# A long convolution with a two-layer MLP: batch 1's second transform stage as four 64x64 products, its spectrum product on VectorE through PSUM, and the pair sums on GpSimd

## The chip, the cores and the metric

The kernel runs on one core of a Trainium2 chip. The metric is the time of one execution on the device in microseconds (us), measured from launch to end. Engines are named as the profile names them: PE (TensorE's matmuls), PEld (its weight loads), DVE (VectorE), ACT (ScalarE), POOL (GpSimd), SP (SyncE, which issues most DMAs here). PSUM is the accumulator memory that PE writes; DVE and ACT read and write it.

## The reference

For two batches of 12480 tokens with 128 channels it computes a causal convolution along the sequence with a filter made by a small MLP from position embeddings, multiplies by x, and runs a two-layer MLP over all 24960 tokens:

```python
h_filt = (np.maximum(pos_emb @ w1, 0.0) @ w2) * window
u = x * v
y = np.fft.irfft(np.fft.rfft(u, n=2*S, axis=1) * np.fft.rfft(h_filt, n=2*S, axis=0), n=2*S, axis=1)[:, :S]
a = (x * y).reshape(B * S, D)
h = a @ w_in
out = np.maximum(0.01 * h, h) @ w_out
```

## The kernel before

**The convolution** is a two-stage Fourier transform over a sequence of 98 x 128 points. Stage one works along 98 points (matmuls with tables `ft`), stage two along 128 points, which `mb` splits into two halves s = 0, 1 of 64 outputs each. Stage two works on 25 *chunks* of up to four frequencies k (4 x 128 channels = 512 columns; the 13th chunk falls into two pieces, the last has 256 columns). In each chunk the forward transform gives the spectrum, it is multiplied by the filter's spectrum `hspec`, and an inverse transform along the same axis gives `ct`, which goes to DRAM (`scr2`). The last inverse stage is part of the MLP's front: for a pair of rows (a *tile* t of 390 tokens) `join_hi` (L673) and `join_lo` (L687) form sums and differences `cp`, matmuls `yp` (L933) transform them, and transposes, products with x and a split into a high and a low part make the MLP's input `zh`, `zl`.

**Order of the program.** Batch 0 goes through its two stages first (to about 340 us). Then the MLP runs in *slots*: 50 column blocks k times 16 blocks f of the hidden layer, 800 slots. In each slot `m1` issues three matmuls (L1009, a high and low split in place of one fp32 product) into one of three PSUM banks `mh`; ACT makes `rh` (L1013), DVE makes `rl` (L1014), and `m2`, three slots later, issues three matmuls (L1050 to L1052). Every engine runs its own instructions in the order in which the program issues them.

**Batch 1's convolution is laid between the MLP's slots.** `conv1` (stage one) and `conv1b` (stage two) are generators; after each slot `pace` calls them for as many *pieces* as a straight line asks for, so that they end a few slots before batch 1's first tile. So each `yield` in `conv1b` is a place where MLP instructions come between. Before, one chunk of `conv1b` has 15 pieces, about 1.5 a slot, and a chunk comes every 9 to 10 slots.

**One chunk of `conv1b` before.** The input is split into a high part (ACT, L507 and L511, `th`) and a low part (DVE, L512, `tl`). The forward transform takes six matmuls of the full array (L150 in `three`: for each s, high by high, low by high, high by low) into two PSUM banks `cv` that are obtained by `psc["next"]`. ACT copies both banks with the halves exchanged (L551, L558), DVE multiplies the banks by `hspec`'s real part (L553), POOL multiplies the exchanged copy by the imaginary part and adds (L517, L518). ACT and POOL split the product again (L575 `ph`, L576 `pl`). One chunk later `back` issues six more matmuls (L150) into the same two banks, and ACT copies the result out (L230 in `mixed_evac`). There are only two `cv` buffers, so a chunk's inverse transform, the other user, can start only when the forward result of the chunk in hand has been read.

`join_hi` forms the upper-half sums of a pair with DVE for t = 0 and for batch 0's tiles from 8 on, and with POOL for the others.

Of the kernel before, what the change touches and what calls it, by code (L numbers as in the profile page):

```python
# [8 lines left out]
F32 = mybir.dt.float32  # L9
F32R = mybir.dt.float32r  # L10
# [11 lines left out]
MC1 = 4  # L22
# [8 lines left out]
def tile_conv_mlp(ctx, tc, x, v, pos_emb, w1, w2, w_in, w_out, cf, cr, cg, cb, ci, cw, out):  # L31
# [20 lines left out]
    hspec = dram.tile([NCH, HB, 2, 2, 512], F32, name="hspec")  # L52
# [11 lines left out]
    mb_h = const.tile([128, 2, 128], F32R, name="mb_h")  # L64
    mb_l = const.tile([128, 2, 128], F32R, name="mb_l")
    mi2 = [const.tile([128, 2, 128], F32, name=f"mi2{j}") for j in range(2)]
    mi_h = [const.tile([128, 2, 128], F32R, name=f"mi_h{j}") for j in range(2)]
    mi_l = [const.tile([128, 2, 128], F32R, name=f"mi_l{j}") for j in range(2)]
# [78 lines left out]
    def three(dst, a, b):  # L147

        for i, (u, w) in enumerate(((a[0], b[0]), (a[0], b[1]), (a[1], b[0]))):
            nc.tensor.matmul(dst, u, w, start=(i == 0), stop=(i == 2))  # L150
# [16 lines left out]
    def even(w):  # L167

        return (w.stop - w.start) // D % 2 == 0

    def back(dp, parts, c):

        for s in range(2):
            for j, w in halves(c):
                m = mixed if even(w) else lambda t: t
                three(dp[s][:, w], (mi_h[j][:, s], mi_l[j][:, s]), (m(parts[0][:, s, w]), m(parts[1][:, s, w])))

    def turned(pool, psum, m2, m1):
# [36 lines left out]
        nc.scalar.copy(mi_h[1], rp[:, 2:4])  # L215
        nc.vector.tensor_tensor(out=mi_l[1], in0=rp[:, 2:4], in1=mi_h[1], op=ALU.subtract)
        yield

    def store_back(b, c, ct, eng):
        k0, n = chunk(c)  # L220
        eng.dma_start(out=scr2[b][k0:k0 + n].rearrange("k r m e -> (r m) k e"),
                          in_=ct[:, :n].rearrange("p k s d -> p k (s d)"))

    def mixed_evac(dp, ct, c):

        for s in range(2):
            for _, w in halves(c):
                o, i = ct[:, w.start // D:w.stop // D, s, :], dp[s][:, w]
                if even(w):
                    nc.scalar.copy(o.rearrange("p (h k) d -> p h k d", h=2),  # L230
                                   i.rearrange("p (k d h) -> p h k d", h=2, d=D))
                else:
                    nc.scalar.copy(o, i.rearrange("p (k d) -> p k d", d=D))
            yield
# [8 lines left out]
    with tc.manual_schedule():  # L243
# [22 lines left out]
        with ExitStack() as st:  # L266
# [86 lines left out]
            for c in range(NC0):  # L353
# [4 lines left out]
                if c == 2:  # L358
                    turn_ = turned(sba, lambda: psa.tile([128, 4, 128], F32, tag="pp", name="tp"), mi2[0], mi)
                    next(turn_)  # L360
                    nc.sync.dma_start(out=mb, in_=cb)
                    nc.sync.dma_start(out=mi, in_=ci)
# [3 lines left out]
                if c == 6:  # L366
                    nc.scalar.mul(mi, mi, 1 / 0.99)
                    for m, mh, ml in ((mb.rearrange("p s r q -> p s (r q)"), mb_h, mb_l), (mi, mi_h[0], mi_l[0])):
                        nc.scalar.copy(mh, m)
                        nc.vector.tensor_tensor(out=ml, in0=m, in1=mh, op=ALU.subtract)  # L370
# [60 lines left out]
        WAIT = 12  # L431
# [49 lines left out]
        def conv1b():  # L481
# [4 lines left out]
            def fetch_b(c):  # L486
                if c < NCH:
# [3 lines left out]
                    nc.sync.dma_start(out=got[c][:, :n].rearrange("p k s d -> p k (s d)"),  # L491
                                      in_=scr1b[:, k0:k0 + n, :])

            def fetch_h(c):
                n = chunk(c)[1]
                h = pool.tile([128, 2, 2, 512], F32, tag="hd", name="hd")
                for i in range(2):
                    nc.sync.dma_start(out=h[HB * i:HB * i + HB, :, :, :n * D], in_=hspec[c][:, :, :, :n * D])
                hd[c] = h

            def split(c):
                _, n = chunk(c)
                t = got.pop(c)
                th = pool.tile([128, KC, 2, D], F32R, tag="th", name="th", bufs=1)
                tl = pool.tile([128, KC, 2, D], F32R, tag="tl", name="tl", bufs=1)
                parts[c] = th, tl
# [810 lines left out]
```

## Time and profile before

| what | value |
|---|---|
| median of 3 runs | 1619.28 us (1616.59 to 1620.77) |
| profiled execution, its own time | 1622.39 us |
| its span, first to last instruction | 1620.6 us |
| PE busy | 1559.0 us, 96% of the span |
| DVE, ACT, POOL busy | 70%, 61%, 46% |
| mean granted clock of TensorE | 0.986 |

Busy time is the union of an engine's instructions. A matmul's record is longer than the distance to the next one, since matmuls are pipelined: the distances between their starts tell what PE is paid for.

### The profile page before, as it was taken

To read this page: it belongs to the slowest core of one execution; us is meant where nothing else is said; L and a number is where in the kernel's file an instruction comes from. 1 tells how busy PE (TensorE), PEld (TensorE's weight loads), DVE (VectorE), ACT (ScalarE), POOL (GpSimd) and SP (SyncE) were. 2 spreads that over 40 slices of the span, in tenths; PEclk is the share of its full clock that TensorE was granted. 3 is DMA by queue.
4 is the path that set the end of the run, shared out by engine and by line. 5 is a ranking of instruction groups with operands and counts; after the bars stand their busy time and mean duration, and the time that the engine had idled before them with its cause. 6 is when DMAs were issued, how large, how long until landed. Compare 5 with 4: busy or idle time off the path is not lost.

```text
span 1620.6 us, 27366 instructions
## 1 busy us (share of the span) xinstructions
PE 1559.0 (96%) x9173; PEld 1323.7 (82%) x9173; DVE 1129.5 (70%) x1785; ACT 995.9 (61%) x2108; POOL 748.6 (46%) x804
## 2 busy tenths in 40 slices
PE   6798899899999999999999999999999999999999
PEld 6787555478888888888888888988888888888888
DVE  4676687765777566666677775577777777777777
ACT  2232454435655466777776777677777776777776
POOL 4563121234735257677777775453433533334310
PEclk9899999999999999999999999999999999999999
DMA  8898999966676557666656752321212212122200
GB/s 247 266 297 264 309 318 324 326 177 200 199 200 200 154 155 195 192 181 181 170 164 179 194 141 63 110 95 57 77 58 63 68 63 87 58 63 62 63 11 21
DMA packets 166358, 253.31 MB, mean 156 GB/s; under 512 B 14302, under 2 KB 119026, under 8 KB 163146
## 3 DMA queue, kind: packets, MB, share of 16 engines
q1 hardware_dynamic: 146478, 226.29, 47.2%
q10 hardware_dynamic: 19740, 25.28, 4.6%
q8 instruction: 73, 1.20, 0.3%
q14 instruction: 67, 0.55, 0.1%
HBM read 168.00 MB, written 83.43 MB: 155 GB/s over the span
## 4 chain that ended last, share of the span: by engine, by line
PE 74%; DMA 9%; DVE 6%; ACT 3%; issue 2%; SPq 1%; POOL 1%; ACTq 0%; DVEq 0%; POOLq 0%
PE mh L1009 28%; PE acc L1051 9%; PE acc L1052 9%; PE acc L1050 9%; PE yp L933 4%; PE cv L150 3%; PE cv L454 3%; DMA scr<-ct 3%; PE op L1082 2%; PE zp L952 1%; PE up L136 1%; DMA pos<-in_pos_emb_dram 1%; PE dp L164 1%; DMA scr<-o 1%; PE a L410 1%
## 5 line engine op out<-in xcount | busy, mean ns | idle before, releaser
L1014 DVE SCALAR_TENSOR_TENSOR rl<-mh,rh 128x512 fp32r<-128x512 f32 (+1 forms) x336 | 226.7, 682 | 199.1 <-ACT rh L1013 197.9
L1022 DVE TENSOR_TENSOR rl<-mh,rh 128x512 fp32r<-128x512 f32 (+2 forms) x416 | 277.2, 670 | 83.6 <-ACT rh L1021 75.0
L1017 ACT ACTIVATE mh<-mh 128x512 f32<-128x512 f32 (+2 forms) x416 | 236.3, 568 | 154.0 <-PE mh L1009 113.3
L1009 PE MATMUL mh<-zh,w_in_h 128*128 128x512 f32 (+3 forms) x800 | 316.8, 396 | 3.6 <-DVE rl L1014 2.4
L1009 PE MATMUL mh<-zl,w_in_h 128*128 128x512 f32 (+3 forms) x800 | 300.0, 375 | 0.2 <-POOL zl L966 0.2
L1009 PE MATMUL mh<-zh,w_in_l 128*128 128x512 f32 (+3 forms) x800 | 299.6, 375 | 0.0
L1051 PE MATMUL acc<-rl,w_out_h 128*128 128x512 f32 (+3 forms) x800 | 299.1, 374 | 0.1
L1050 PE MATMUL acc<-rh,w_out_h 128*128 128x512 f32 (+3 forms) x800 | 299.0, 374 | 0.0
L1052 PE MATMUL acc<-rh,w_out_l 128*128 128x512 f32 (+3 forms) x800 | 299.0, 374 | 0.0
L1013 ACT ACTIVATE rh<-mh 128x512 fp32r<-128x512 f32 (+1 forms) x336 | 198.9, 595 | 133.1 <-PE mh L1009 124.3
L966 POOL TENSOR_TENSOR zl<-zf,zh 128x390 fp32r<-128x390 f32 (+24 forms) x110 | 67.8, 630 | 426.5 <-ACT zh L965 403.8
L696 POOL TENSOR_TENSOR cp<-cq,cp 98x256 f32<-98x256 f32 x248 | 194.0, 782 | 32.6 <-DVE cp L684 15.9
L1019 DVE CAST rh<-mh 128x512 fp32r<-128x512 f32 (+2 forms) x208 | 139.3, 670 | 65.9 <-ACT mh L1017 65.5
L1009 PEld LDWEIGHTS mh<-zh,w_in_h 128*128 128x128 f32 x800 | 151.7, 190 | 29.6 <-DVE rl L1014 8.7
L1009 PEld LDWEIGHTS mh<-zh,w_in_l 128*128 128x128 f32 x800 | 151.8, 190 | 19.7
L1051 PEld LDWEIGHTS acc<-rl,w_out_h 128*128 128x128 f32 x800 | 151.2, 189 | 20.2 <-DVE rl L1022 0.4
L1050 PEld LDWEIGHTS acc<-rh,w_out_h 128*128 128x128 f32 x800 | 151.2, 189 | 19.8
L1052 PEld LDWEIGHTS acc<-rh,w_out_l 128*128 128x128 f32 x800 | 151.2, 189 | 19.7
L1009 PEld LDWEIGHTS mh<-zl,w_in_h 128*128 128x128 f32 x800 | 152.2, 190 | 15.6 <-POOL zl L966 0.6
L1021 ACT CAST rh<-mh 128x512 fp32r<-128x512 f32 (+2 forms) x208 | 118.5, 570 | 6.5
L693 POOL TENSOR_TENSOR cq<-cin 98x256 f32<-98x256 f32 x124 | 97.6, 787 | 0.3 <-DMA cin<-scr 0.3
L105 ACT COPY a1s<-a 98x384 f32<-98x384 f32 x64 | 30.7, 480 | 97.3 <-PE a L410 68.7
(170 smaller groups left out, 2529.8 us busy)
## 6 DMA issues: line engine op xcount, KB each, us to landing
cin<-scr SPq DMA_DIRECT2D x318, 98.0 KB
hd<-hspec SPq DMA_DIRECT2D x48, 512.0 KB
bin<-scr SPq DMA_DIRECT2D x23, 768.0 KB
scr<-o SPq DMA_DIRECT2D x28, 588.0 KB
scr<-ct SPq DMA_DIRECT2D x25, 512.0 KB
scr1b<-o SPq DMA_DIRECT2D x32, 392.0 KB
hspec<-hs ACTq DMA_DIRECT2D x48, 256.0 KB
xm<-in_x_dram SPq DMA_DIRECT2D x128, 96.0 KB
```

Of the source, the lines that this page charges most:

```text
L693: eng.tensor_tensor(out=cq[:, p], in0=ci_t[:, 0, :, 0, :], in1=ci_t[:, 0, :, 1, :], op=op)
L696: eng.tensor_tensor(out=cp[:, p, w], in0=cq[:, p], in1=cp[:, p, 1], op=op)
L1009: nc.tensor.matmul(hp, u[:, fs], m, start=(i == 0), stop=(i == 2))
L1013: nc.scalar.activation(out=split2(rh), in_=plain(hp), func=AF.Relu)
L1014: nc.vector.scalar_tensor_tensor(out=split2(rl), in0=plain(hp), scalar=0.0, in1=split2(rh), op0=ALU.max, op1=ALU.subtract)
L1017: nc.scalar.activation(out=hp, in_=hp, func=AF.Lrelu, alpha=0.01)
L1019: nc.vector.tensor_copy(split2(rh), plain(hp))
L1021: nc.scalar.copy(split2(rh), plain(hp))
L1022: nc.vector.tensor_tensor(out=split2(rl), in0=plain(hp), in1=split2(rh), op=ALU.subtract)
L1050: nc.tensor.matmul(ap, w_out_h[:, f, :], rh, start=(f == 0 and not sums(k)), stop=False)
L1051: nc.tensor.matmul(ap, w_out_h[:, f, :], rl, start=False, stop=False)
L1052: nc.tensor.matmul(ap, w_out_l[:, f, :], rh, start=False, stop=(f == NF - 1))
```

## The change

In `conv1b` the split into high and low parts is gone. The input of a chunk is loaded with its even rows in partitions 0 to 63 and its odd rows in 64 to 127. `fwd2` multiplies each by a 64x64 table `mt` in plain fp32, four matmuls: an even and an odd bank, each with both halves s. ACT copies the odd bank to SBUF (`odd`), DVE forms difference and sum back into the two PSUM banks, and then four products with `hspec`, read from PSUM: `p1` with the real part, `q` with the imaginary part. ACT copies `q` into `jq` with the halves exchanged, in four pieces of 32 partitions by 1024; POOL adds `jq` to `p1` one chunk later and forms sum and difference `pin`. `back2` then issues four matmuls of 64x64 (two chunks after the forward transform), and ACT copies the result out. A chunk has 24 pieces in place of 15. `hspec`'s layout, its loads (four DMAs for two), the input's load and the store (two DMAs for one each) follow. `join_hi` uses POOL for every t but 0. Set-up forms the tables `mt` and `bt` in place of the split ones.

```diff
+    def fwd2(up, t, n):
+        for s in range(2):
+            for e in range(2):
+                r = slice(HB * e, HB * e + HB)
+                nc.tensor.matmul(up[e][HB * s:HB * s + HB, :n * D].rearrange("p (k d) -> p k d", d=D),
+                                 mt[r, s, :], t[r, :n, s, :], start=True, stop=True)
+    def back2(dp, pin, c):
+        for j, w in halves(c):
+            for s in range(2):
+                r = slice(HB * s, HB * s + HB)
+                for e in range(2):
+                    nc.tensor.matmul(dp[s][HB * e:HB * e + HB, w], bt[j][r, e::2], pin[r, e, w],
+                                     start=True, stop=True)
...
-        WAIT = 12
+        WAIT = 24
+        LAST_B = 6
...
+            for c in range(NCH + 2):
...
+                    fwd2(up, t, n)
+                    yield
+                    odd = pool.tile([128, 1024], F32, tag="pl", name="odd", bufs=1)[:, :w]
+                    q = pool.tile([128, 2, 512], F32, tag="th", name="q", bufs=1)
+                    nc.scalar.copy(odd, up[1][:, :w])
+                    yield
+                    for i, op in ((1, ALU.subtract), (0, ALU.add)):
+                        nc.vector.tensor_tensor(out=up[i][:, :w], in0=up[0][:, :w], in1=odd, op=op)
+                        yield from rest(2)
...
+                for i in range(2):
+                    if 0 < c <= NCH:
+                        nc.gpsimd.tensor_tensor(out=o1[:, i, :v], in0=o1[:, i, :v], in1=jq[:, i, :v], op=ALU.add)
                         yield
+                    if c < NCH:
+                        for r, t in ((1, q), (0, p1)):
+                            nc.vector.tensor_tensor(out=t[:, i, :w], in0=up[i][:, :w], in1=h[:, i, r, :w], op=ALU.mult)
+                            yield from rest(2)
...
+                if c > 1:
                     dp = psc["next"]()
+                    back2(dp, pin, c - 2)
+                    yield
+                    ct = cts[c % 2]
+                    yield from back_evac(dp, ct, chunk(c - 2)[1])
+                    late = lambda c=c, ct=ct: store_back(1, c - 2, ct, nc.sync)
...
+                for i in range(4):
+                    if 0 < c <= NCH and i % 2 == 0:
+                        nc.gpsimd.tensor_tensor(out=pin[:, i // 2, :v], in0=o1[:, 0, :v], in1=o1[:, 1, :v],
+                                                op=ALU.subtract if i else ALU.add)
+                    if c < NCH:
+                        o = 32 * (i ^ 1)
+                        if i % 2:
+                            nc.scalar.copy(jq[32 * i:32 * i + 32, :, :w], q[o:o + 32, :, :w])
+                        else:
+                            nc.scalar.mul(jq[32 * i:32 * i + 32, :, :w], q[o:o + 32, :, :w], -1.0)
+                    if c <= NCH:
+                        yield
...
-            eng = nc.vector if t == 0 or 8 <= t < NT else nc.gpsimd
+            eng = nc.vector if t == 0 else nc.gpsimd
```

How the instructions stand is shown at three places; [waits ...] names the engine (or DMA queue) whose signal a row waits for. On PE before, an inverse transform in the middle of `conv1b` (`cv`, six matmuls between two slots):

```order
L1009 MATMUL mh_9126<-zh_8621,w_in_h_67 128x512 [waits DVE_49]
L1009 MATMUL mh_9126<-zl_8622,w_in_h_67 128x512
L1009 MATMUL mh_9126<-zh_8621,w_in_l_68 128x512
L1050 MATMUL acc_9066<-rh_9062,w_out_h_69 128x512 [waits Activation_49]
L1051 MATMUL acc_9066<-rl_9063,w_out_h_69 128x512
L1052 MATMUL acc_9066<-rh_9062,w_out_l_70 128x512
L150 MATMUL cv_9144<-ph_8861,mi_h1_78 128x512 [waits Activation_49]
L150 MATMUL cv_9144<-pl_8862,mi_h1_78 128x512 [waits Pool_49]
L150 MATMUL cv_9144<-ph_8861,mi_l1_80 128x512
L150 MATMUL cv_9143<-ph_8861,mi_h1_78 128x512 [waits DVE_49]
```

On DVE before, around the same slots; the row of `cv_9027` is the read that frees the bank of `cv_9143`:

```order
L553 TENSOR_TENSOR usp_9034<-cv_9026,hd_8823 128x512 [waits DMAHW4_49,DMAHW5_49,PE_49,Pool_49]
L1014 SCALAR_TENSOR_TENSOR rl_9044<-mh_9039,rh_9043 128x512 [waits Activation_49]
L1014 SCALAR_TENSOR_TENSOR rl_9063<-mh_9058,rh_9062 128x512 [waits Activation_49]
L553 TENSOR_TENSOR usp_9034<-cv_9027,hd_8823 128x512
L1014 SCALAR_TENSOR_TENSOR rl_9084<-mh_9079,rh_9083 128x512 [waits DVE_49,Activation_49]
L512 TENSOR_TENSOR tl_9101<-bin1_8740,th_9100 128x4x128 [waits DMAHW0_49,Activation_49]
L1014 SCALAR_TENSOR_TENSOR rl_9110<-mh_9105,rh_9109 128x512 [waits DVE_49,Activation_49]
L512 TENSOR_TENSOR tl_9101<-bin1_8740,th_9100 128x4x128
L1014 SCALAR_TENSOR_TENSOR rl_9131<-mh_9126,rh_9130 128x512 [waits DVE_49,Activation_49]
```

The inverse transform stands behind the slot of `mh_9126`, so the `rl` of three slots (`mh_9079`, `mh_9105`, `mh_9126`) lie between the read that frees the bank and the matmuls that write it. After the change, an inverse transform (`cv_8226`, `cv_8225`) on PE:

```order
L1013 MATMUL mh_8210<-zh_7552,w_in_h_67 128x512 [waits DVE_49]
L1013 MATMUL mh_8210<-zl_7553,w_in_h_67 128x512
L1013 MATMUL mh_8210<-zh_7552,w_in_l_68 128x512
L1054 MATMUL acc_7975<-rh_8169,w_out_h_69 128x512 [waits Activation_49]
L1055 MATMUL acc_7975<-rl_8170,w_out_h_69 128x512
L1056 MATMUL acc_7975<-rh_8169,w_out_l_70 128x512
L180 MATMUL cv_8226<-pins_5950,bt0_76 64x512 [waits DVE_49]
L180 MATMUL cv_8226<-pins_5950,bt0_76 64x512 [waits Pool_49]
L180 MATMUL cv_8225<-pins_5950,bt0_76 64x512 [waits DVE_49]
L180 MATMUL cv_8225<-pins_5950,bt0_76 64x512
```

Four matmuls of 64 rows stand in the place of six full ones. Their DVE waits are for the rows that read the same PSUM buffers last: `p1s<-cv_8093` (even bank of the chunk in hand) frees that of `cv_8226`, and `p1s<-cv_8092` (odd bank) that of `cv_8225`. On DVE after, these rows:

```order
L1018 SCALAR_TENSOR_TENSOR rl_8186<-mh_8181,rh_8185 128x512 [waits Activation_49]
L556 TENSOR_TENSOR p1s_5949<-cv_8093,hd_7870 128x512 [waits Pool_49]
L1018 SCALAR_TENSOR_TENSOR rl_8201<-mh_8196,rh_8200 128x512 [waits Activation_49]
L556 TENSOR_TENSOR q_8099<-cv_8092,hd_7870 128x512
L556 TENSOR_TENSOR p1s_5949<-cv_8092,hd_7870 128x512
L1018 SCALAR_TENSOR_TENSOR rl_8215<-mh_8210,rh_8214 128x512 [waits Activation_49]
L1018 SCALAR_TENSOR_TENSOR rl_8236<-mh_8231,rh_8235 128x512 [waits Activation_49]
```

The read that frees the second bank now stands behind the `rl` of `mh_8196`, and the inverse transform behind the slot of `mh_8210`: the matmuls of one slot lie between, where there were three. Over the whole program 25 inverse transforms before had two to four slots between. After, 23 follow a product: in 4 the last product stands behind the `rl` of the very slot that precedes the inverse; in 19 one slot earlier, as above, and in 7 of these both products of the odd bank stand behind the same `rl`, as above, in 12 only one.

On ACT after, the rows behind the inverse transform:

```order
L1017 ACTIVATE rh_8235<-mh_8231 128x512 [waits DVE_49,PE_49]
L236 COPY ct1_5951<-cv_8226 128x4x128 [waits DMAHW4_49,DMAHW3_49]
L236 COPY ct1_5951<-cv_8225 128x4x128
L580 ACTIVATE jq_8247<-q_8099 32x1024 [waits DVE_49,Pool_49]
L1017 ACTIVATE rh_8254<-mh_8250 128x512 [waits PE_49,Activation_49]
L578 COPY jq_8247<-q_8099 32x1024
L580 ACTIVATE jq_8247<-q_8099 32x1024
L1017 ACTIVATE rh_8270<-mh_8266 128x512 [waits PE_49,Activation_49]
L578 COPY jq_8247<-q_8099 32x1024
L1017 ACTIVATE rh_8296<-mh_8292 128x512 [waits PE_49,Activation_49]
```

The two copies of the inverse's banks and the four copies of `q` stand behind three `rh` in a row, three of them behind the first. Behind the inverse transform shown of before, the two copies of its banks (L230) and the next two of `ph` (L575) each had an `rh` behind them.

## Rows read from the trace of the kernel before

**Rows 1.** The page, part 1: span, and busy time of each engine.
```profile
span 1620.6 us, 27366 instructions
PE 1559.0 (96%) x9173; PEld 1323.7 (82%) x9173; DVE 1129.5 (70%) x1785; ACT 995.9 (61%) x2108; POOL 748.6 (46%) x804
```
**Rows 2.** Windows: stretch, length, busy (count) per engine, PE's granted clock, DMA share, GB/s.
```profile
580.00:1005.00 425.00, 420.12 (x2239) 361.39 (x2238) 285.52 (x393) 308.79 (x644) 304.68 (x294) 1.00 0.60 169
```
**Rows 3.** Waits of PE, 580 to 1010 us: total, times, longest, in us.
```profile
PE mh L1009 <- DVE rl L1014: 2.4, 5, 0.8
PE cv L150 <- ACT ct L230: 1.8, 1, 1.8
```
**Rows 4.** The chain of waits around 695 us: start, us, what.
```profile
695.69 3.19 DVE cp L684 x2
698.88 1.20 DVE tl L512 x2
```
**Rows 5.** Timeline of PE, an inverse transform and the next slot: start, us, instruction.
```profile
748.33 0.38 PE L150 MATMUL cv<-pl,mi_h 128*128 128x512 f32 x1
...
749.41 0.38 PE L1009 MATMUL mh<-zh,w_in_h 128*128 128x512 f32 x1
```
**Rows 6.** Timeline of PE where small matmuls (98 by 64) come between full ones.
```profile
1134.42 0.38 PE L1052 MATMUL acc<-rh,w_out_l 128*128 128x512 f32 x1
1134.73 1.97 PE L933 MATMUL yp<-cp,gt 98*64 98x128 f32 x32
1136.63 0.48 PE L1009 MATMUL mh<-zh,w_in_h 128*128 128x512 f32 x1
1136.95 0.38 PE L1009 MATMUL mh<-zl,w_in_h 128*128 128x512 f32 x1
```
**Rows 7.** Timelines of PE, batch 0's second stage (plain fp32, half the array each).
```profile
259.74 0.65 PE L136 MATMUL up<-bin,mb 128*64 128x512 f32 x2 [0.20 <-DVE ta L144]
260.19 0.63 PE L136 MATMUL up<-bin,mb 128*64 128x512 f32 x2
...
261.05 0.63 PE L136 MATMUL up<-bin,mb 128*64 128x512 f32 x2
...
209.31 0.60 PE L164 MATMUL dp<-pin,mi 64*128 64x512 f32 x2
```
**Rows 8.** Lines of DVE, 580 to 1005 us: count, busy, mean ns, idle before.
```profile
L512 DVE TENSOR_TENSOR tl<-bin,th 128x512 fp32r<-128x512 f32 (+1 forms) x50 | 59.0, 1194 | 0.6 <-ACT th L507 0.6
L553 DVE TENSOR_TENSOR usp<-cv,hd 128x512 f32<-128x512 f32 (+1 forms) x50 | 33.6, 673 | 7.9 <-ACT usp L558 4.9 <-PE cv L150 1.8 <-DMA hd<-hspec 0.9
L684 DVE TENSOR_TENSOR cp<-cin 98x256 f32<-98x256 f32 x36 | 32.5, 915 | 0.0
```
**Rows 9.** Lines of ACT, 580 to 1005 us; the last two by shape, whole execution.
```profile
L230 ACT COPY ct<-cv 128x512 f32<-128x512 f32 x45 | 25.6, 588 | 13.6 <-DMA scr<-ct 8.2 <-PE cv L150 4.5 <-PE mh L1009 0.8
...
L507 ACT CAST th<-bin 128x512 fp32r<-128x512 f32 x24 | 14.8, 617 | 0.2
L741 ACT CAST w_in_h<-wi 128x256 fp32r<-128x256 f32 x8 | 3.2, 405 | 3.5 <-ACT ct L239 0.9 <-DVE tb L144 0.9 <-DVE ta L144 0.9
```
**Rows 10.** Lines of POOL, 580 to 1005 us; the last by shape, whole execution.
```profile
L517 POOL TENSOR_TENSOR usp<-usp,hd 128x512 f32<-128x512 f32 (+1 forms) x50 | 64.9, 1298 | 22.3 <-ACT usp L558 15.1 <-DMA cin<-scr 7.1
...
L684 POOL TENSOR_TENSOR cp<-cin 98x256 f32<-98x256 f32 x78 | 56.0, 738 | 67.4 <-PE yp L933 31.9 <-DMA gt<-in_cg_dram 16.1 <-PE yp L981 14.6
```
**Rows 11.** Timeline of all engines at one slot: start, us, instruction, idle before and its cause.
```profile
734.64 0.41 DVE L684 TENSOR_TENSOR cp<-cin 98x256 f32<-98x256 f32 x1
...
734.97 0.38 PE L1050 MATMUL acc<-rh,w_out_h 128*128 128x512 f32 x1
...
735.17 0.60 ACT L1013 ACTIVATE rh<-mh 128x512 fp32r<-128x512 f32 x1 [0.81 <-PE mh L1009]
...
735.80 0.69 DVE L1014 SCALAR_TENSOR_TENSOR rl<-mh,rh 128x512 fp32r<-128x512 f32 x1 [0.75 <-ACT rh L1013]
```
**Rows 12.** Waits of SP's queue, 580 to 1005 us: total, times, longest, in us.
```profile
SPq L498 <- POOL usp L517: 34.6, 10, 7.2
```

More of the change, by code (lines that the diff above doesn't have):

```diff
@@ L145, in product, with quads @@
             e.tensor_tensor(out=pin[:, o, :w], in0=ta[:, o, :w], in1=tb[:, q, :w], op=op)
-    def three(dst, a, b):
-        for i, (u, w) in enumerate(((a[0], b[0]), (a[0], b[1]), (a[1], b[0]))):
-            nc.tensor.matmul(dst, u, w, start=(i == 0), stop=(i == 2))
+    def quads(dst, src):
+        for s in range(2):
+            for r in range(2):
+                nc.scalar.copy(dst[HB * s + 32 * r:HB * s + 32 * r + 32, :], src[HB * r:HB * r + 32, s, :])
     def halves(c):
@@ L220, in store_back @@
         k0, n = chunk(c)
+        if b:
+            for e in range(2):
+                eng.dma_start(out=scr2[b][k0:k0 + n].rearrange("k r (m e) d -> e (r m) k d", e=2)[e],
+                              in_=ct[HB * e:HB * e + HB, :n].rearrange("p k s d -> p k (s d)"))
+            return
         eng.dma_start(out=scr2[b][k0:k0 + n].rearrange("k r m e -> (r m) k e"),
                           in_=ct[:, :n].rearrange("p k s d -> p k (s d)"))
[L224 to L234, printed above, removed]
     def back_evac(dp, ct, n):
@@ L496, in fetch_h @@
                 h = pool.tile([128, 2, 2, 512], F32, tag="hd", name="hd")
-                for i in range(2):
-                    nc.sync.dma_start(out=h[HB * i:HB * i + HB, :, :, :n * D], in_=hspec[c][:, :, :, :n * D])
-                hd[c] = h
[L501 to L506, printed above, removed]
-                nc.scalar.copy(th[:, :n, 0, :], t[:, :n, 0, :])
-                yield
-                for s in range(2):
-                    if s == 0:
-                        nc.scalar.copy(th[:, :n, 1, :], t[:, :n, 1, :])
-                    nc.vector.tensor_tensor(out=tl[:, :n, s, :], in0=t[:, :n, s, :], in1=th[:, :n, s, :],
-                                            op=ALU.subtract)
-                    yield
@@ L525, in conv1b, with rest @@
                 yield
-            yield from split(0)
-            late, pins = None, {}
-            for c in range(NCH + 1):
+            late, held = None, {}
+            p1s, pins = (sc.tile([128, 2048], F32, tag="s4", name=g).rearrange("a (i h w) -> i a h w", i=2, h=2)
+                         for g in ("p1s", "pins"))
+            pin = pins[0]
+            cts = [pins[1].rearrange("p h (k d) -> p (h k) d", d=D).rearrange("p (k s) d -> p k s d", s=2),
+                   pool.tile([128, KC, 2, D], F32, tag="ct1", name="ct1", bufs=1)]
+            def rest(n):
+                for _ in range(n):
+                    yield
+            for c in range(NCH + 2):
                 if c + 1 < NCH:
@@ L536, in conv1b @@
                     w = n * D
-                    h, (th, tl) = hd.pop(c), parts.pop(c)
+                    h, t = hd.pop(c), got.pop(c)
+                    p1 = p1s[c % 2]
                     yield
                     up = psc["next"]()
-                    for s in range(2):
-                        three(up[s][:, :w], (mb_h[:, s], mb_l[:, s]),
-                              [i[:, :n, s, :].rearrange("p (h k) d -> p k d h", h=2) for i in (th, tl)])
+                    fwd2(up, t, n)
                     yield
-                    us, p1 = sc.tile([128, 2048], F32, tag="s4", name="usp").rearrange(
-                        "a (i s w) -> i a s w", i=2, s=2)
```

87 lines of the change are left out of this document (34 added, 53 removed).

## The prediction

> **What bounds the kernel now.** The page's first part comes first: PE is busy 96% of the span, DVE 70%, ACT 61%, POOL 46% [rows 1]. The windows then say where the change lies. Batch 1's second stage, `conv1b`, runs from about 580 to 1005 us (the first and the last of its lines), and there PE is busy 420.12 of 425.00 us at the full clock of 2.4 GHz (granted 1.00) [rows 2]. So an engine other than PE can cost this stretch only through PE, and the reader should keep two sums apart: what PE's own work costs, and PE's 4.9 us of waiting. The waits name their two large parts, `mh` waiting for `rl` (2.4 us) and the inverse transform waiting for the copy `ct` (1.8 us) [rows 3]. The chain of waits shows how the first comes about: at 695 us DVE is 3.19 us in two sums of `join_hi` and 1.20 us in a `tl`, while `rl` stands behind them [rows 4]. Batch 0's second stage, before 340 us, keeps its matmuls.
>
> **PE's own work.** Six of `conv1b`'s full matmuls of 512 columns follow each other at 0.216 us (five steps from 748.33 to 749.41) [rows 5], so the twelve of a full chunk take 2.59 us. The eight that replace them are plain fp32 on quarters of the array, in two groups of four. No row shows a quarter. The nearest are batch 0's halves: a pair of halves (marked x2) takes a step of 0.45, then 0.43 us (259.74, 260.19; 261.05 is two steps on) [rows 7], and one fp32 product takes two such steps, so a group costs 0.88 us if all four quarters run side by side. Changing from full to small matmuls and back costs too: `yp` starts 0.31 us after the matmul ahead of it, not 0.22 (0.09 more), and the first matmul behind the small ones takes 0.32 us to the next, not 0.22 (0.10 more) [rows 6]; I add 0.10 for the gap ahead of that one. A group is then 0.09 + 0.88 + 0.20 = 1.17 us, two are 2.34, and a chunk gains 0.25 us. With 23 full chunks that is **−5.7** us; the two short ones are left at nothing. The other bound is that only two quarters run at once, as halves do: each group then takes 0.88 us more, 48 groups +42 us. I take four: the halves split by rows (64*128) [rows 7] and those split by columns both run in pairs, so each direction splits.
>
> The Trainium skill (TensorEngine Tiling (Array Packing), Tiling Modes) lists 64x64 as four independent tiles and says that a change of mode drains the engine. The gaps around `yp` [rows 6] agree with the drain, and no run here shows four tiles at once; by this page the group costs what I took.
>
> **What goes from the old waits.** `tl` (50 of 1.194 us) and the DVE form of L684 (36 of 0.915 us) leave DVE's stretch [rows 8]. Both have been the long ones: an L684 elsewhere takes 0.41 us [rows 11], and the product L553, which reads PSUM, takes 0.673. The second `ct` buffer removes the wait for `ct`. Of 4.9 us up to all may go; I take **−4.4**.
>
> **The new wait on DVE.** This is the largest term. The inverse transform takes over the PSUM banks of the chunk in hand, now read last by DVE's products (L556). Before, the `rl` of three slots lay between that read and the inverse (two to four over the program); the order of instructions after has one slot between in 19 chunks and none in 4. When is the product done? In the slot at 735 us, `m1`'s third matmul is handed over to the next at 734.97, `rh` starts at 735.17, `rl` at 735.80 for 0.69: `rl` ends 1.52 us after the handover, with nothing in the way [rows 11]. A product takes 0.69 us, between L553's 0.673 and the 1.194 of `tl` [rows 8], near the first since it too reads one operand from PSUM; I add 0.05 for the signal. PE reaches the inverse's second pair, which needs the odd bank, 9 × 0.216 + 0.09 = 2.03 us after the handover with one slot between, and 3 × 0.216 + 0.09 = 0.74 with none. Three cases follow:
> - one slot, one product behind `rl` (12 chunks): 1.52 + 0.05 + 0.69 = 2.26, a wait of 0.23, together 2.8 us;
> - one slot, both products behind it (7): 2.95, a wait of 0.92, together 6.4 us;
> - no slot, one product (4): 2.26 against 0.74, a wait of 1.52, together 6.1 us.
>
> That is 15.3 us, and since other work of PE (transposes, `yp`) lies between in some, 13 as the floor of this reading. If an ACT copy of 0.59 us (the mean of L230) [rows 9] stands ahead of `rh`, every case with a wait grows by it: 23 × 0.59 = 13.6 more, up to 29. The lower bound is that PE runs behind anyway, because `m1` itself waits; then only the 4 chunks without a slot pay, 6 us. I take **+15**, near the row that I trust. What is queued behind the waiting matmul on PE is the next slot's `m1`, hence `rh` and `rl`: nothing of it can be made up, since PE has no idle time to give back.
>
> The Trainium skill (TensorEngine Tiling (Array Packing), PSUM Bottleneck) says that tiling speeds up TensorE but not the emptying of PSUM, which may become the bottleneck. It speaks against this change and fits the term above: matmuls save 6 us and the reads of their banks decide the rest. The trace before shows the like only in the 1.8 us wait for `ct` [rows 3].
>
> **The new burst on ACT.** Behind an inverse ACT now has two copies of banks, 0.59 us each, and four copies of 32 partitions by 1024 within three slots. No row has 1024 columns; 512 take 0.617 us and 256 take 0.405 [rows 9], 0.212 for each 256 columns, so I estimate 0.617 + 2 × 0.212 = 1.04 us. From one `rh` to the end of the next but one ACT has 0.60 + 0.59 + 0.59 + 1.04 + 0.60 + 1.04 + 1.04 + 0.60 = 6.1 us; PE gives it 2.6 us of two slots and 0.6 for the last `rh`, so that `rh` comes 2.9 us late. An `mh` bank is needed again 15 matmuls and an inverse later, 15 × 0.216 + 1.17 = 4.4 us, and it is free 1.52 + 2.9 = 4.4 us after its own. It just fits; about 0.4 us of wait in half of the chunks is **+4**, with 0 and 14 (0.6 in each of 23) as ends. A chunk's sum on ACT hardly changes: eight passes of 0.6 and two of `ct` go, and `odd` (one of 0.6), two of `ct` and four of 1.04 come.
>
> **Edits at nothing.** POOL loses six operations of 1.3 us a chunk (L517, L518, L576; L517's mean [rows 10]) and gets four; with 48 upper sums of 0.738 us it is less busy than now, and PE's two large waits [rows 3] are not for it. If that cover were gone, a late sum would hold back `yp`; its price is the 0.738. SP issues eight DMAs a chunk for four, of the same bytes; its queue now spends 34.6 us blocked on POOL's L517 [rows 12], a reason that goes. The set-up trades two small splits for two table loads; I take 0, with ±3 in the range.
>
> **Sum.** −5.7 − 4.4 + 15 + 4 = +8.9 us on the profiled execution's 1622.4 us (span 1620.6 [rows 1] and 1.8 around it). That execution is 3.1 us above the median of 1619.3, so I forecast 1628 us, **slower**, with a range of its own from 1624 to 1645 (at DVE's upper bound, +29 for +15, it is 1642).
>
> **Rivals.**
> 1. *The waits are hidden, faster.* DVE's busy time in the stretch falls: 285.5 − 59.0 − 33.6 − 32.5 + 25 × 6 × 0.69 = 264 us, and without the long operations `rl` follows `rh` at once. If only the four chunks without a slot wait, −5.7 − 4.4 + 6 = −4.1, about 1615; with no wait of either kind, old ones too, −5.7 − 4.9 = −10.6, 1608.7. It decides where the new waits sum to less than 10.1 us, 0.44 us a chunk (by over 0.3% where they are under 5). Against it: 1.52 us is already the undisturbed lag.
> 2. *Two quarters at a time.* −5.7 + 42 − 4.4 + 2 (PE, slower itself, waits less): +34, 1653 us. For it: rows 7 show two and never four. Against it: both directions split.
> 3. *Nothing to measure.* The same mechanisms with waits of 5 to 15 us, 1614.4 to 1624.2. I take 0.3%, 4.9 us, as what can be told from no change.
>
> **How the numbers follow.** Forecast (slower by over 0.3%, quarters side by side) 0.41, rival 2 0.09, rival 3 0.18, rival 1 (by over 0.3%) 0.32. So faster 0.32, same 0.18, slower 0.50. The range reaches down to rival 1's end with no waits and the set-up's 3 us, 1606, and up to 1650, short of both upper bounds of the new waits together (−5.7 − 4.4 + 29 + 14 = +33, 1652); outside lie rival 2 and gains larger than the old waits allow.
>
> **What the changed profile would show.** The four matmuls of a group start within 0.1 us and repeat once 0.43 us later, else rival 2. PE's waits list the inverse (L180) behind `p1s` (L556) with 8 to 29 us, else rival 1. The copies L578 and L580 take 1.0 us, and `mh` behind `rl` stays at about 4 us; if they run at half that, this term is nothing. L556 and L545 take about 0.69 us; were L545, which also writes PSUM, much slower, the products come later and the DVE term grows by the excess. The forecast is wrong if PE's start after a group costs more than 0.2 us, or if the gaps in 340 to 580 or behind 1005 us change, where I expect none.

## The result and the profile after

The changed kernel takes 1641.91 us (median of 5 runs, 1639.86 to 1644.82) against 1619.28 us before (1616.59 to 1622.34): a ratio of 1.0142, with a 95% interval from 1.0123 to 1.0162. It is slower, by 22.6 us where 8.7 were forecast. The profiled execution is one of 1641.91 us; its span is 19.4 us longer than that of before, since the profiled execution of before was 3.1 us above its median. First the page's first part, then the window of the stretch (columns as in [rows 2]):

```profile
span 1640.0 us, 27651 instructions
PE 1574.3 (96%) x9275; PEld 1280.2 (78%) x9275; DVE 1088.5 (66%) x1784; ACT 1005.3 (61%) x2036; POOL 699.2 (43%) x802
```

```profile
580.00:1005.00 425.00, 415.35 (x2241) 304.27 (x2240) 243.57 (x389) 299.89 (x539) 235.54 (x270) 1.00 0.64 165
```

DVE and POOL have become lighter, as the change says, and PE is still busy 96% of a longer span. That busy time misleads here. The stretch is where the time went: from the first matmul of slot 100 to that of slot 400 it is 521.4 us before (530.0 to 1051.4) and 542.0 after (528.8 to 1070.8), 20.6 us more; the slots 0 to 100 and those from 400 on take the same within 0.5 us. The waits of PE from 570 to 1050 us, beside [rows 3]:

```profile
PE mh L1013 <- DVE rl L1018: 4.3, 7, 1.2
PE cv L180 <- DVE p1s L556: 4.0, 6, 1.3
PE op L1086 <- ACT ot L1073: 1.3, 1, 1.3
PE cv L180 <- ACT pins L236: 0.7, 1, 0.7
```

These sum to 10.3 us, of which 4.0 are the new wait, where the forecast wanted 8 to 29. But the view counts a wait only where no matmul is on record, and an inverse that waits halfway is half on record. The lines of PE in the stretch show it:

```profile
L1013 PE MATMUL mh<-zh,w_in_h 128*128 128x512 f32 x225 | 95.3, 424 | 4.6 <-DVE rl L1018 4.3
L180 PE MATMUL cv<-pins,bt 64*64 64x512 f32 (+2 forms) x184 | 40.7, 597 | 5.0 <-DVE p1s L556 4.0 <-ACT pins L236 0.7
L171 PE MATMUL cv<-bin,mt 64*64 64x512 f32 x192 | 26.1, 615 | 0.0
```

Forward (L171) and inverse (L180) transforms are eight such records a group, but for one inverse in two pieces (16 shorter records, the 13th chunk). The 24 forward groups are busy 26.1 us, 1.09 each; the 22 inverse groups of this window take 40.7 + 5.0 us, 2.08 each: 0.99 × 22 = 21.8 us too much. The timeline of PE shows one group of each kind:

```profile
746.27 0.38 PE L1056 MATMUL acc<-rh,w_out_l 128*128 128x512 f32 x1
746.68 1.08 PE L180 MATMUL cv<-pins,bt 64*64 64x512 f32 x4
749.07 1.08 PE L180 MATMUL cv<-pins,bt 64*64 64x512 f32 x4 [1.31 <-DVE p1s L556]
750.08 0.48 PE L1013 MATMUL mh<-zh,w_in_h 128*128 128x512 f32 x1
...
755.94 0.38 PE L1056 MATMUL acc<-rh,w_out_l 128*128 128x512 f32 x1
756.25 1.09 PE L171 MATMUL cv<-bin,mt 64*64 64x512 f32 x8
757.27 0.48 PE L1013 MATMUL mh<-zh,w_in_h 128*128 128x512 f32 x1
757.59 0.38 PE L1013 MATMUL mh<-zl,w_in_h 128*128 128x512 f32 x1
```

The forward group issues its eight records without a wait (four within 0.02 us, four more 0.48 us later), and the next `mh` starts 1.02 us after its first; every one of the 24 does. The inverse at 746.68 issues four, and the other four start only 2.39 us after its first, when `p1s` is done; its next `mh` comes 3.40 us after its first. I call what a group takes beyond 1.02 us (0.60 for the short one) its **stretch**. Added up over all inverses, from the starts of the matmuls, it is 21.7 us. By the three cases of the forecast: one slot and one product (12 chunks), 7.5 us; one slot and two products (7), 7.3; no slot (4), 7.0. One of the twelve, at 875.84 us, is not of this kind: its last product ends 0.18 us after the group's first start, but its second half starts after 1.76 us, and the profile names ACT's copy (L236) of the group's own first bank. That is 1.5 us of the 21.7 (and again in number 9 below).

DVE at that inverse, and ACT ahead of it, in their timelines:

```profile
737.53 0.69 DVE L1018 SCALAR_TENSOR_TENSOR rl<-mh,rh 128x512 fp32r<-128x512 f32 x1 [3.32 <-ACT rh L1017]
740.28 0.69 DVE L1018 SCALAR_TENSOR_TENSOR rl<-mh,rh 128x512 fp32r<-128x512 f32 x1 [2.06 <-ACT rh L1017]
...
742.35 0.69 DVE L545 TENSOR_TENSOR cv<-cv,odd 128x512 f32<-128x512 f32 x1
742.95 0.68 DVE L1018 SCALAR_TENSOR_TENSOR rl<-mh,rh 128x512 fp32r<-128x512 f32 x1
743.55 0.69 DVE L545 TENSOR_TENSOR cv<-cv,odd 128x512 f32<-128x512 f32 x1
...
747.73 0.68 DVE L1018 SCALAR_TENSOR_TENSOR rl<-mh,rh 128x512 fp32r<-128x512 f32 x1
748.33 0.68 DVE L556 TENSOR_TENSOR p1s<-cv,hd 128x512 f32<-128x512 f32 x1
```

```profile
735.83 1.04 ACT L578 COPY jq<-q 32x1024 f32<-32x1024 f32 x1
736.90 0.60 ACT L1017 ACTIVATE rh<-mh 128x512 fp32r<-128x512 f32 x1
737.52 1.05 ACT L580 ACTIVATE jq<-q 32x1024 f32<-32x1024 f32 x1
738.59 1.04 ACT L578 COPY jq<-q 32x1024 f32<-32x1024 f32 x1
739.65 0.60 ACT L1017 ACTIVATE rh<-mh 128x512 fp32r<-128x512 f32 x1
740.15 0.58 ACT L1099 COPY os<-op 98x512 f32<-98x512 f32 x1
740.62 0.60 ACT L542 COPY odd<-cv 128x512 f32<-128x512 f32 x1
```

Read ACT first and then DVE: ACT is in the copies `jq` of the chunk before, then in `os` (a copy of the MLP's output) and `odd`; DVE has nothing for 3.32 and 2.06 us since `rh` is late; then its six operations on the chunk and the `rl` between them follow each other without a gap, a start every 0.60 us, up to the `p1s` at 748.33 for which PE waits.

### The profile page after: what moved, and what is told of

It reads as the page before. It is cut to its first block, busy times and chain, and to the rows that moved or that the text cites. A ratio compares the mean times of both kernels' runs of the same rounds, so it can differ in the third digit from the quotient of the medians.

```text
span 1640.0 us, 27651 instructions
## 1 busy us (share of the span) xinstructions
PE 1574.3 (96%) x9275; PEld 1280.2 (78%) x9275; DVE 1088.5 (66%) x1784; ACT 1005.3 (61%) x2036; POOL 699.2 (43%) x802
## 4 chain that ended last, share of the span: by engine, by line
PE 70%; DMA 10%; DVE 8%; ACT 6%; issue 3%; SPq 1%; POOL 1%; ACTq 0%; DVEq 0%; POOLq 0%
PE mh L1013 27%; PE acc L1055 9%; PE acc L1056 9%; PE acc L1054 9%; PE yp L937 4%; PE cv L453 3%; PE cv L180 2%; DMA scr<-o 2%; DMA hspec<-hs 2%; DMA pos<-in_pos_emb_dram 2%; PE op L1086 2%; DVE rl L1018 2%; ACT jq L578 2%; PE zp L956 1%; DMA vt<-in_v_dram 1%
## 5 line engine op out<-in xcount | busy, mean ns | idle before, releaser
L1013 PE MATMUL mh<-zh,w_in_h 128*128 128x512 f32 (+3 forms) x800 | 322.4, 403 | 5.3 <-DVE rl L1018 4.3
L700 POOL TENSOR_TENSOR cp<-cq,cp 98x256 f32<-98x256 f32 x248 | 188.5, 760 | 16.5
L1013 PEld LDWEIGHTS mh<-zl,w_in_h 128*128 128x128 f32 x800 | 152.3, 190 | 13.7 <-DVE zl L1002 0.2
L688 POOL TENSOR_TENSOR cp<-cin 98x256 f32<-98x256 f32 x126 | 92.1, 747 | 83.8 <-PE yp L937 36.9
```

Source lines behind the costliest of these rows:

```text
L700: eng.tensor_tensor(out=cp[:, p, w], in0=cq[:, p], in1=cp[:, p, 1], op=op)
L1013: nc.tensor.matmul(hp, u[:, fs], m, start=(i == 0), stop=(i == 2))
```

## The experiments

All ratios are to the kernel before, with runs of it on the same chip; its medians there were 1617.3 to 1619.0 us. Intervals are 95%.

**1. Products earlier** (and an inverse two slots behind them in every chunk).

```diff
                             nc.vector.tensor_tensor(out=t[:, i, :w], in0=up[i][:, :w], in1=h[:, i, r, :w], op=ALU.mult)
-                            yield from rest(2)
+                            yield from rest(1)
                 if c < NCH:
                     fetch_b(c + 3)
+                    yield from rest(4)
```

> Changed kernel, with the four products of a chunk one piece apart instead of two and the four pieces so won put between the last product and the inverse transform: two slots lie between the two in every chunk (zero or one before), the number of pieces is the same. Theory A, the inverse waits for DVE's last product behind rl: the 21 stretched inverse groups (each lasts 1.1 to 3.4 us from its first start to the next mh, 1.02 where nothing holds it) go back to about 1.02, which takes 20 to 21 us off: about 1621 us, and PE's wait for p1s L556 goes to under 1 us. Theory B, half of the stretch is the matmuls' own (the quarters of the inverse run two and two, 0.48 us later, as the groups at 694.84 and 730.46 do): only what exceeds 1.49 us goes, about 11 us: 1631 us, and third starts stay at 0.48. Theory C, the lost time is not tied to that read at all (ACT's burst or DMA): no change, 1642 us.

Measured: 1625.79 us, 1.0045 (1.0030 to 1.0061), 16 us off. The timeline of PE at an inverse, and the lines of the stretch:

```profile
689.38 1.09 PE L180 MATMUL cv<-pins,bt 64*64 64x512 f32 x8
690.41 0.48 PE L1014 MATMUL mh<-zh,w_in_h 128*128 128x512 f32 x1
```

```profile
L1014 PE MATMUL mh<-zh,w_in_h 128*128 128x512 f32 x234 | 99.1, 424 | 5.3 <-DVE rl L1019 4.8
L180 PE MATMUL cv<-pins,bt 64*64 64x512 f32 (+2 forms) x192 | 29.8, 598 | 0.5 <-DVE p1s L556 0.5
```

The stretch is 5.2 us; 15 of the 24 inverses of 512 columns take the bare 1.02, with no wait inside. Theory A holds in the main, B falls: inverses also run on four quarters at once. Not all of the 20 us came back, and the waits of `mh` for `rl` stay at 4.8.

**2 and 3. The pair sums.** In 2 the changed kernel has them on DVE again, in 3 the kernel before has them on POOL:

```diff
-            eng = nc.vector if t == 0 else nc.gpsimd
+            eng = nc.vector if t == 0 or 8 <= t < NT else nc.gpsimd
```

(in 3 the other way round).

> Changed kernel with the upper-half sums of batch 0's tiles from 8 on back on DVE (36 of them in the stretch of the second stage). Theory A, DVE's chain behind rl sets the inverse's wait: sums of 0.4 to 0.9 us each in DVE's queue delay it further where they fall close, 2 to 8 us longer than the changed kernel, 1644 to 1650 us. Theory D, the sums on POOL are what costs (cp late for yp, or POOL slower for pins): 2 to 5 us shorter, 1637 to 1640 us.

> Kernel before with only the upper-half sums moved from DVE to POOL. Theory A: the waits of mh for rl (2.4 us, two sums and a tl on DVE at 695 us) shrink, nothing else changes: 0 to 3 us shorter than before, 1616 to 1619 us. Theory D: POOL, with six operations of 1.3 us a chunk here, falls behind, and yp or the inverse waits for it: 2 to 10 us longer, 1621 to 1629 us.

Measured: 2 takes 1651.61 us, 1.0205 (1.0185 to 1.0224), 10 us more than the changed kernel; its stretch is 29.9 us, 8.2 more. 3 takes 1618.65 us, 0.9995 (0.9982 to 1.0007): no change. So this part of the change gains nothing in the kernel before, and 10 us once the other part is in: 36 sums of 0.69 us stand in a queue for whose end PE waits. Theory A in both, a little above its range in 2.

**4. ACT's copies apart.** Two pieces apart instead of one, the pieces taken between DVE's first four operations:

```diff
                         nc.vector.tensor_tensor(out=up[i][:, :w], in0=up[0][:, :w], in1=odd, op=op)
-                        yield from rest(2)
+                        yield from rest(1)
...
                             nc.vector.tensor_tensor(out=t[:, i, :w], in0=up[i][:, :w], in1=h[:, i, r, :w], op=ALU.mult)
-                            yield from rest(2)
+                            yield from rest(1 + i)
...
                             nc.scalar.mul(jq[32 * i:32 * i + 32, :, :w], q[o:o + 32, :, :w], -1.0)
                     if c <= NCH:
-                        yield
+                        yield from rest(2 if c < NCH else 1)
```

> Changed kernel with ACT's four copies of q two pieces apart instead of one, the four pieces taken between DVE's operations ahead of the last two products; the distance from the last product to the inverse is as in the changed kernel (none in 2 chunks instead of 4, one slot in the others). Theory A, the burst on ACT costs little by itself (waits of mh for rl 4.3 us, of op for ot 1.7 us): these fall by 2 to 4 us, and two chunks fewer without a slot give 2 to 3 us: 1635 to 1639 us. Theory C, copies ahead of rh are what makes rl and with it the products late: the stretch of the inverses falls by 10 us or more, 1625 to 1632 us.

Measured: 1642.66 us, 1.0159 (1.0137 to 1.0181), the same as the changed kernel. Both expectations missed. The waits of `mh` for `rl` fell from 4.3 to 1.2 us and that of `op` went, but the stretch rose to 26.8 us. Lateness left one place and came out at the other, which made me doubt that the two waits are two things.

**5. Both** (the edits of 1, and copies two pieces apart; 28 pieces a chunk).

> Changed kernel with the products one piece apart, four pieces between the last product and the inverse, and ACT's four copies of q two pieces apart; a chunk then has 28 pieces. One slot lies between last product and inverse in 7 chunks, two in 16. Theory A (two terms that add: the inverse's wait behind rl, and ACT's burst, which is now in the waits of mh for rl, 4.8 us, and of op for ot, 1.3 us): the stretch of the inverses stays at 5 to 9 us (21 in the changed kernel, 5 with the products earlier alone), the other waits go: 1620 to 1625 us, at or under the kernel with the products earlier alone (1626). Theory C, the two are one queue (copies later on ACT push rh and the products of the next inverse): 1628 us or more.

Measured: 1627.76 us, 1.0056 (1.0042 to 1.0070). The waits of `mh` halved (2.1 us), the stretch is 13.7 us, above the 5 to 9 expected; between the two theories, nearer C.

**6. The products `q` first**, so that the copies can begin ahead of the inverse (27 pieces a chunk).

```diff
+                    prod(1, 0, q)
+                    yield from rest(2)
+                    prod(1, 1, q)
+                    yield from rest(2)
...
+                    prod(0, 0, p1)
+                    yield
+                    turn(0)
+                    yield
+                    prod(0, 1, p1)
+                    yield
+                    for i in range(1, 4):
+                        turn(i)
+                        yield from rest(2)
```

(`prod` is the product L556, `turn` one of the four copies.)

> Changed kernel with the two products q ahead of the two p1, the first of ACT's copies of q put behind the first p1 and the other three, two pieces apart, between the last product and the inverse; a chunk has 27 pieces, and two slots (12 chunks) or three (11) lie between last product and inverse. Theory A: the stretch of the inverses goes to under 2 us, ACT's burst is spread ahead of the inverse and off its own copies; what is left is the 5 us that the quarters of the array save and the 2 us wait that the second ct buffer took away, less 2 us: 1612 to 1617 us, under the kernel before (1618.5). Theory C, ACT's copies ahead of the inverse make rh late, and mh waits for rl instead: 1620 to 1628 us.

Measured: 1613.88 us, 0.9972 (0.9961 to 0.9982): faster than both kernels. The waits of PE, 570 to 1050 us, whole:

```profile
PE cv L171 <- ACT ct L236: 1.0, 2, 0.8
PE cv L171 <- ACT pins L236: 0.7, 2, 0.5
```

No wait for DVE is left, and the inverses' stretch is 0.4 us. In its place the full forward groups are stretched by 5.6 us and held up by 2.1 us ahead of their first start (they wait for the copies of the inverse's banks).

**7. Number 6 with the sums on DVE again.**

> The kernel with the products q first (1613.9 us), with the upper-half sums of batch 0's tiles from 8 on back on DVE. Theory A, the sums cost where the inverse waits for DVE's queue, and there alone: with two or three slots between last product and inverse that distance takes most of the delay, so 0 to 4 us longer, 1614 to 1618 us (in the changed kernel the same edit cost 9.7). Theory E, the sums cost by themselves (DVE's operations on two SBUF operands are slow and hold up rl wherever they stand): 7 us or more, 1621 us or more.

Measured: 1618.78 us, 1.0003 (0.9989 to 1.0017), 5 us more than number 6 and half of what the edit costs in 2; the stretch of the inverses is 0.8 us. Nearer A, but above its range: the sums' price here does not go through the inverses' wait. Of the 3.0 us that the slots 100 to 400 take longer than in number 6, 1.5 are at the forward groups, 0.6 ahead of `mh` and 0.4 at the inverses, by the starts on PE.

**8. Number 6 with the burst back**: the four copies behind the inverse, one piece apart; two or three slots still lie between the last product and the inverse (29 pieces a chunk).

> The kernel with the products q first, with ACT's four copies of q put back behind the inverse, one piece apart, as in the changed kernel; two slots (16 chunks) or three (7) still lie between last product and inverse. This prices the burst alone. Theory A: the waits of mh for rl and of op for ot come back, 4 to 7 us together, and the inverses are hardly stretched (under 3 us): 1617 to 1622 us. Theory C, the copies ahead of the inverse were no help by themselves and the order of the products did it all: 1613 to 1615 us.

Measured: 1628.15 us, 1.0068 (1.0047 to 1.0089), 14 us more than number 6, above both ranges. Its first two waits of PE:

```profile
PE mh L1026 <- DVE rl L1031: 7.0, 8, 1.5
PE cv L180 <- POOL pins L590: 2.1, 1, 2.1
```

The stretch is 4.8 us, 3.3 of it at the one inverse that waits for POOL. So the burst costs 14 us (11.9 in the slots 100 to 400) even where the inverse is well behind the products, most of it through `rl`: the steps into `mh` exceed 0.216 us by 10.4 us in all, and by 0.2 in number 6.

**9. The changed kernel with short copies**, no instruction moved. Each copy of `q` and each of POOL's adds takes 128 of 512 columns; the imaginary part is left out for the others.

```diff
-                            nc.scalar.copy(jq[32 * i:32 * i + 32, :, :w], q[o:o + 32, :, :w])
+                            nc.scalar.copy(jq[32 * i:32 * i + 32, :, :128], q[o:o + 32, :, :128])
```

(the other copy and the add alike)

> Changed kernel with its order of instructions as it is, but each of ACT's four copies of q takes 128 of the 512 columns of either half (32x256, about 0.4 us where it is 1.05 now), and POOL's adds take the same 128 columns: the imaginary part is left out for the rest of the columns, and POOL is busy for less. Theory F (one chain: the burst holds up rh, DVE starts its six operations on the chunk late, and since rl and one such operation take 1.20 us of a slot of 1.29 it never catches up, so the next inverse waits): the stretch of the inverses falls from 21 us to under 12 with no instruction moved, the waits of mh for rl go too, 1622 to 1628 us. Theory A (two terms that add: the inverse waits because it stands too close behind the last product, burst or not): the stretch stays at 15 us or more, the waits of mh for rl (4.3 us) go: 1633 to 1638 us.

Measured: 1625.84 us, 1.0036 (1.0021 to 1.0051), 16 us off. Lines of PE and, in a fence of its own, ACT:

```profile
L1013 PE MATMUL mh<-zh,w_in_h 128*128 128x512 f32 x233 | 97.1, 417 | 0.0
L180 PE MATMUL cv<-pins,bt 64*64 64x512 f32 (+2 forms) x192 | 38.8, 597 | 2.9 <-DVE p1s L556 2.0 <-ACT pins L236 0.7
L171 PE MATMUL cv<-bin,mt 64*64 64x512 f32 (+1 forms) x200 | 26.8, 606 | 0.0
```

```profile
L580 ACT ACTIVATE jq<-q 32x256 f32<-32x256 f32 x48 | 19.9, 414 | 1.0
L578 ACT COPY jq<-q 32x256 f32<-32x256 f32 x48 | 19.3, 402 | 0.8
```

The time is that of theory F, the stretch that of theory A: 16.7 us, with the waits of `mh` gone. By cases it is 1.49 us a chunk with no slot (forecast 1.52), 0.88 with one slot and two products (0.92), 0.38 with one slot and one product (0.23; 0.26 if the inverse that waits for ACT's copy is put at 0.23). So without the burst the inverses wait what the undisturbed chain `rh`, `rl`, product predicts, and the burst adds 5 us to that and 10 us elsewhere, 7.0 of them ahead of `mh`. POOL's shorter adds are part of the edit; no wait for POOL had been listed in the stretch of the changed kernel.

PE has the same instructions in the same order in both kernels, so the loss can be read chunk by chunk, from the end of one inverse to the end of the next. In 13 chunks the MLP's other operations on ACT (`zf` and `zh` for its input, `ot` and `os` for its output) stand within the burst, that is, between the `rh` ahead of the bank copies and the `rh` behind the last `jq`; they take 13.1 us of ACT's time, and these chunks lose 16.1 us against number 9. In the 10 whose burst has none the sum is −1.2 us, −1.7 in one and at most 0.3 in any other. POOL's adds are shorter in all of them alike.

**10 and 11. Trying to gain the forward groups' 5.6 us back.** In 10 (27 pieces a chunk) three of the copies come before or beside the two `p1`; 11 has two more pieces ahead of the next forward transform too.

```diff
                     prod(1, 1, q)
+                    yield
...
+                    turn(0)
+                    yield
                     prod(0, 0, p1)
+                    yield
+                    turn(1)
+                    yield
                     prod(0, 1, p1)
+                    yield
+                    turn(2)
+                    yield from rest(2)
+                    turn(3)
+                    yield from rest(4)
...
                     held[c] = jq_
+                    if c > 1:
+                        yield from rest(2)
```

(the last two lines in 11 alone)

> The kernel with the products q first, with ACT's copies of q started directly behind the second q, so that three of the four stand before or beside the p1 products and the last ends four pieces ahead of the inverse. In the kernel with q first the forward groups are stretched by 5.6 us in all and two waits for the inverse's bank copies (1.0 and 0.7 us) are listed: the copies on ACT push the bank copies back. Theory: with the copies earlier the bank copies start on time, 2 to 5 us off, 1609 to 1612 us; rival: rh is pushed ahead of the last product instead, and the stretch goes back to the inverses, 1614 to 1620 us.

> The same with two more pieces between the inverse's bank copies and the next forward transform (29 pieces a chunk). Theory: the forward groups' stretch of 5.6 us goes, with nothing new: 1608 to 1611 us; rival: DVE's six operations get less of a chunk and the inverses stretch again: 1613 us or more.

Measured: 10 takes 1619.64 us, 1.0018 (1.0000 to 1.0036), 11 takes 1628.59, 1.0071 (1.0054 to 1.0088): the rivals. The forward stretch went to 1.6 and 0.5 us, but the inverses' rose to 4.8 and 9.4, and `mh` waits for `rl` again, 3.6 and 5.9 us.

## Why the prediction went wrong

The direction and the mechanism of the largest term were right; the change is 22.6 us where I had 8.7, mainly since one term was put at 4 us and costs 15. In the working's own order, for the 300 slots from 100 to 400 (predicted, then measured; the waits from the starts of PE's matmuls, which see more than the list of waits does):

- **PE's own work**, −5.7: the right sign, a third too large. A group is 0.10 + 1.02 + 0.10 = 1.22 us, not 1.17, since its second four records follow after 0.48 us and not 0.43. So a full chunk gains 0.15 us and 23 of them 3.5; the two short chunks, which I had left at nothing, give 0.3 together, and the groups right behind a `yp` or `zp` 0.5: −4.3. The Trainium skill (TensorEngine Tiling (Array Packing), Tiling Modes) has 64x64 as four independent tiles: the trace agrees, four records start within 0.02 us and eight take 1.02 us. Rival 2 falls.
- **The old waits**, −4.4: twice that. By starts the steps into `mh` exceed 0.216 us by 4.6 us in the kernel before (by 0.2 in numbers 6 and 9), the step behind a late `mh` is longer too, 1.5 in all, the wait for `ct` is 2.5, and 0.6 lies in the first forward and the last inverse: −9.
- **The new wait on DVE**, +15: right. Number 9 has 16.7 us, of which 15.2 by the mechanism that I had, case by case as forecast, and 1.5 at the one inverse that waits for ACT's copy. The Trainium skill (the same page, Performance Considerations, PSUM Bottleneck) says that emptying PSUM may become the bottleneck when matmuls get faster: the trace agrees, PE's own work falls by 4.3 us and it waits 15.2 us for the last read of a bank.
- **The burst on ACT**, +4 with ends 0 and 14: **this is the step that failed**. Shortening the copies takes 16 us off (number 9; 15 of it in these slots, 542.0 against 526.9), and putting the burst back costs 14 (number 8). "It just fits" was the wrong sentence: it holds only where the MLP leaves ACT alone. The copies' own time was right: 1.04 us was estimated, and it is 1.043 and 1.056:

```profile
L580 ACT ACTIVATE jq<-q 32x1024 f32<-32x1024 f32 x46 | 48.6, 1056 | 1.0
L578 ACT COPY jq<-q 32x1024 f32<-32x1024 f32 x46 | 48.0, 1043 | 0.8
```

The four terms now are −4.3 − 9 + 16.7 + 15 = +18 us against the 20.6 measured in these slots. The 15 is itself a difference of two runs; without it the first three give +3.4, and number 9 measures 5.5 (526.9 against 521.4). What is left, 2 us, lies in small waits of other matmuls, 1.0 of it among those of `yp`.

Why the burst costs so much has two parts. The first is in ACT's queue. These are rows of ACT at the burst behind the inverse shown above, and at one that has nothing of the MLP but `rh`:

```profile
751.03 0.60 ACT L1017 ACTIVATE rh<-mh 128x512 fp32r<-128x512 f32 x1 [4.40 <-PE mh L1013]
...
755.05 0.42 ACT L959 COPY zf<-zp 128x98 f32<-128x98 f32 x2 [0.90 <-PE zp L956]
...
758.50 0.60 ACT L1017 ACTIVATE rh<-mh 128x512 fp32r<-128x512 f32 x1
...
788.31 0.60 ACT L1017 ACTIVATE rh<-mh 128x512 fp32r<-128x512 f32 x1 [3.08 <-PE mh L1013]
788.81 1.07 ACT L236 COPY ct<-cv 128x512 f32<-128x512 f32 x2
...
793.59 0.60 ACT L1017 ACTIVATE rh<-mh 128x512 fp32r<-128x512 f32 x1
```

And the chain of waits at the first:

```profile
755.05 0.42 ACT zf L959 x2
755.46 0.25 ACT zf L961
755.71 0.01 issue
755.73 0.61 ACT zh L969 x2
756.34 0.02 issue
756.36 1.04 ACT jq L578
```

From one `rh` to the end of the next but one I had summed 6.1 us. At 788.31 it is 5.88, and that chunk loses nothing against number 9. At 751.03 it is 8.07: `zf` and `zh` (1.28 us) and the 0.90 us that ACT waits for PE's `zp` ahead of them stand in the same queue, and that chunk loses 2.20. My sum had `rh`, the bank copies and the `jq`, and left out the MLP's other work on ACT. With a slack that I had worked out as nothing (4.4 us against 4.4), each such piece, and the idle time ahead of it, is a wait. The 13 chunks of number 9's comparison show it for the whole stretch: 13.1 us of pieces, 16.1 us lost, 1.2 us a chunk where I had 0.4 us in half of the chunks.

The second part is that I took the two waits as terms that add. They share a queue. After a burst `rh` is late, and DVE's operations on the next chunk start late; each stands behind an `rl`, and the two take 1.20 us (two starts at 0.60) of a slot of 6 × 0.216 = 1.29 us. So DVE makes up 0.09 us in a slot, and what it is late at its first operation it mostly still is at the last product. In number 4 the burst was spread and the time stayed: the lateness came out at the inverse instead of at `mh`. In the changed kernel 5 of the 21.7 us are of this kind (21.7 against 16.7). That the make-up rate is what carries it so far is read from the one stretch from 742 to 749 us and argued for the rest, number 4 included.

The last two points of the working:

- **Edits at nothing.** POOL, SP and the set-up: as forecast, the slots before 100 take 188.1 and 187.7 us, and slot 0 starts at 341.9 and 341.1. The sums on POOL were not at nothing once PE waits for DVE's queue: 10 us (numbers 2 and 3).
- **Rival 1** (faster) had its condition right, new waits under 0.44 us a chunk: number 6, another order of the same work, meets it (8.7 us over 25 chunks), and is 0.28% faster than before.

Open is where the rest of number 7's 5 us lies (3.0 of them are in the slots 100 to 400), why one inverse waits for ACT's copy of its own first bank, and why numbers 4 and 5 put the lateness just there; no run took these apart.

## What to carry to other kernels

A wait that divides one group of matmuls hides in the busy time: compare groups of equal work (2.08 against 1.09 us here) before you trust a list of waits. When work is laid between the slots of a loop, add up each engine's whole queue in those slots, the loop's own small operations included; a slack that comes out as zero is a wait for whatever was left out. And look for an engine that needs nearly the whole slot: it hands a delay on, so that two late places may be one. What helped here was to move the producer (the `q` first), so that the copies could start earlier and lie ahead of the inverse; to spread the copies where they stood gained nothing (numbers 4 and 5).

## What was not expected of the hardware

An operation of DVE on 128x512 is on record for 0.68 us, but in an unbroken row one starts every 0.60 us (742.35, 742.95, 743.55). So the means of [rows 8] overstate by 0.08 us what such an operation takes of a full queue. The pair sum on DVE had a mean of 0.915 us before (L684) and 0.694 in number 2 (L688). In the kernel before, the 14 of the 36 sums that have no operation of POOL beside them take 0.41 to 0.42 us each, and each of the 18 longer ones, up to 2.82 us, has one beside it; in number 2, 18 sums have none and take 0.41 to 0.42 again. Which of POOL's operations slow a sum was not tried.
